# Attended values at another address, a regrouped last output, and earlier v sums in a windowed attention and feed-forward kernel

## The chip, the cores and the metric

One core of one Trainium2 chip. The time is the device time of one execution in microseconds (us); the profile is of one such execution, and its span runs from the first to the last instruction. Five engines work from queues of their own: PE (matrix products; its weight loads are listed apart as PEld), DVE, ACT, POOL, and SP, which here only issues DMA transfers.

## The reference

For each of 4 batches and 8 heads, 768 queries of 64 numbers attend to the keys nearer than 16 positions and, beside them, to 24 summaries of blocks of 32 positions (the maximum of the keys, the mean of the values). The result of all heads, 512 numbers per position, goes through a feed-forward layer:

```python
k_sum = k.reshape(B, H, nb, block, D).max(axis=3)
v_sum = v.reshape(B, H, nb, block, D).mean(axis=3)
...
a = a / (np.sum(a, axis=-1, keepdims=True) + 1e-09)
v_all = np.concatenate([v, v_sum], axis=2)
...
h = x @ w_in
r = np.maximum(h, 0.0)
g = s * (r * r) + b
return (g @ w_out).astype(np.float32)
```

`w_in` is 512 x 2048 and `w_out` 2048 x 512; the output has 3072 rows of 512.

## The kernel before, in words

**Chunks.** The 3072 rows are cut into 12 chunks of 256 rows (`T`), three to a batch. A chunk first needs its attention, which gives the attended values, transposed: four tiles of 128 x 256. They are split into an upper part `xh` in a format that the matrix unit takes in one pass, and a lower part `xl`, the rest. Each weight is split likewise into `wh` and `wl`.

**First products** (`hidden`, L460). For each of 16 steps `f` of the hidden layer, 12 products of 128 x 128 weights (stationary) with 128 x 256 attended values (moving): `wl` with `xh`, `wh` with `xl`, `wh` with `xh`, over four parts each. Two steps share a PSUM tile `ph`. The chain behind it (`activate`, `scaled`, `upper_rows`, `lower_rows`) makes `r` on ACT, scales it on POOL (L481), and splits it into `gh` and `gl` on DVE (L219, L492).

**Second products** (`project`, L504). For each step, two halves of rows (`t`, 128 rows each, PSUM tiles `po`), three products each: `gl` or `gh` stationary, 128 x 512 output weights moving. After step 15 `evict` copies each `po` to a tile `o` and sends it out (L514).

**The order of work** is a table `plan`: `then(step, order, ...)` appends a piece to a step of 1/16 chunk, and all engines get their instructions in that order. From chunk 2 on, first products are issued for four steps at once and second products for the four steps before, so PE alternates 48 first products and 24 second products. Each chunk boundary has a visit in which PE makes the values of the next chunk (`values`, L417) and the scores of the one after it (`scores`, L301).

**Sums of v** for the three later batches, made during the chunk before the batch's first: `load_v` brings v in six pieces (L165, SP), `v_sum` adds blocks on DVE (L172), `v_mean` scales on ACT (L178) into `vmean`, of which there is one buffer, and sends it by four small DMAs into `vsum` (L180, SP). `fill_v` on POOL (L263) copies `vsum` into the rows of `vw` that `values` reads. ACT runs its queue in order, and so does each of the others.

**Addresses.** Where tiles lie in a partition of SBUF, in bytes modulo 256, in the built programs of both kernels (the two buffers of a name separated by a comma):

| tile | role in products | before | with the change |
|---|---|---|---|
| xh and xl, each | moving in first products | 0, 0 | 192, 192 |
| wh, wl (rings) | stationary in first, moving in second products | 0 | 0 |
| gh and gl, each four | stationary in second products | 0 | 0 |
| r | between ACT, POOL, DVE | 0, 0 | 192, 224 |
| pr | between DVE and ACT | 192, 224 | 192, 64 |
| pT | moving in `values` | 192, 192 | 192, 192 |
| qk (four) | both sides of `scores` | 0, 160, 64, 224 | the same |

Of the kernel before, what the change touches and what calls it, by code (L numbers as in the profile page):

```python
# [11 lines left out]
F32 = mybir.dt.float32  # L12
# [7 lines left out]
P = 128  # L20
B, H, S, D = 4, 8, 768, 64
DM, DFF = 512, 2048
# [5 lines left out]
KR = WIN + NB  # L28
NSUB = 4
T = NSUB * SUB  # L30
NPAIR = H // 2
PER_B = S // T
NC = B * PER_B
NST = S // SUB
NKC = DM // P
NF = DFF // P
# [8 lines left out]
def windowed_attention_then_relu2_ffn(ctx, tc, qk, vwin, kt, vt, kq, vrow, wp, out):  # L45


    nc = tc.nc
# [4 lines left out]
    stage = ctx.enter_context(tc.tile_pool(name="stage", bufs=4))  # L53
    p2 = ctx.enter_context(tc.tile_pool(name="p2", bufs=2))
# [29 lines left out]
    def mask_of(st):  # L84
        return mask_first if st == 0 else mask_last if st == NST - 2 else mask_mid
# [3 lines left out]
    def at(step, order, fn, *args):  # L89
        plan[step].append((order, len(plan[step]), fn, args))  # L90
# [5 lines left out]
    for base, sign in ((0, 1), (BLOCK - 1, -1)):  # L96
        nc.gpsimd.affine_select(
            out=mean4[:, NB - 4 : NB], in_=mean4[:, NB - 4 : NB], compare_op=ALU.is_ge, fill=0.0,
            base=base, pattern=[[-sign * BLOCK, 4]], channel_multiplier=sign,
# [3 lines left out]
    w_raw, w_f, w_h, w_l, held = {}, {}, {}, {}, {}  # L103
# [113 lines left out]
    def copy(by_dve, out_, in_):  # L217
        if by_dve:
            nc.vector.tensor_copy(out_, in_)  # L219
        else:  # L220
            nc.scalar.copy(out_, in_)  # L221
# [7 lines left out]
    def place(c):  # L229
        return c // PER_B, c % PER_B  # L230
# [75 lines left out]
    def masked(c, p, j):  # L306
        _, ci = place(c)
        if j == 0 and c == 0:
            t = stage.tile([P, 4 * KR + 8], F32, name="pr0", tag="stage")
            pr_of[c, p] = t[:, : 4 * KR].rearrange("p (n k) -> p n k", k=KR)  # L310
            mn_of[c, p], sm_of[c, p] = t[:, 4 * KR : 4 * KR + 4], t[:, 4 * KR + 4 :]
        elif j == 0:
            if (c, p // 2) not in prs_of:
                prs_of[c, p // 2] = p2.tile([P, 8 * KR + 8], F32, name="pr", bufs=2)
                if turns_on_dve(c):
                    nc.gpsimd.memset(prs_of[c, p // 2][:, 8 * KR :], 0.0)
            t = prs_of[c, p // 2][:, 4 * KR * (p % 2) : 4 * KR * (p % 2 + 1)]
            pr_of[c, p] = t.rearrange("p (n k) -> p n k", k=KR)
            mn_of[c, p] = p2.tile([P, 4], F32, name="mn", bufs=4)
            sm_of[c, p] = p2.tile([P, 4], F32, name="sums", bufs=4)  # L320
        for e in range(2):
            n = 2 * e + j
            nc.vector.tensor_tensor_reduce(  # L323
                out=pr_of[c, p][:, n, :], in0=ps_of[c, p][e][:, j, :], in1=mask_of(NSUB * ci + 2 * j),
                scale=-1.0 / math.sqrt(D), scalar=3.0e38, op0=ALU.add, op1=ALU.min,
                accum_out=mn_of[c, p][:, n : n + 1],
            )
        if j == 1:
            ps_of.pop((c, p))
            qk_t.pop((c, p))  # L330
# [17 lines left out]
    prs_of, pTs_of = {}, {}  # L348

    def turns_on_dve(c):  # L350
        return c > 2
# [84 lines left out]
    ph_of, gg, po = {}, {}, {}  # L436
# [25 lines left out]
            )  # L462

    def activate(c, q, other=0):
        gg[c, q] = r = p2.tile([P, 2 * T], F32, name="r")
        ph = ph_of.pop((c, q))
        if other < 2:
            nc.scalar.activation(r, ph, AF.Relu)  # L468
        else:
            nc.vector.tensor_scalar(r, ph, 0.0, None, ALU.max)  # L470
        if other % 2:
            nc.vector.tensor_tensor(r, r, r, ALU.mult)
        else:
            nc.scalar.activation(r, r, AF.Square)  # L474
# [20 lines left out]
    def project(c, f):  # L495
        if f == 0:
            for t in range(T // P):
                pool, tag = ((ps_t, "pt"), (ps_v, "pav"))[t] if c == 1 else (ps_po, "po")
                po[c, t] = pool.tile([P, DM], F32, name="po", tag=tag)
        gh, gl = (g[:, (f % 2) * T : (f % 2 + 1) * T] for g in gg[c, f // 2])  # L500
        terms = [(gl, w_h[f]), (gh, w_l[f]), (gh, w_h[f])]
        for t in range(T // P):
            for n, (a, w) in enumerate(terms):
                nc.tensor.matmul(  # L504
                    po[c, t], a[:, t * P : (t + 1) * P], w[:, 512:],
                    start=(f == 0 and n == 0), stop=(f == NF - 1 and n == len(terms) - 1),
                )

    def evict(c, t, other=False):
        o = stage.tile([P, DM], F32, name="o", tag="stage")  # L510
        copy(other, o, po[c, t])
        bi, ci = place(c)
        r0 = bi * S + ci * T + t * P
        nc.sync.dma_start(out[r0 : r0 + P, :], o)  # L514


    LOAD, SPLIT, ATT, NEXT, TURN, WEIGHTS, HID, PE_ATT, CHAIN, VISIT, PROJ, EVICT = range(12)
# [29 lines left out]
    def of(fn, *more):  # L547
# [4 lines left out]
        "i": of(load_weights, "in"), "o": of(load_weights, "out"), "w": of(load_weights, "in", "out"),  # L552
        "u": load_unit, "x": load_values, "L": load_k,
        "W": keep_warm, "K": k_max, "k": fill_k, "Z": scores_of_maxima, "S": scores, "M": masked, "E": exps,
        "N": normalize, "T": transposes, "C": turned, "V": values, "U": values_of_means, "R": mean_of_rows,
        "F": mean_done, "t": fill_v, "X": attended, "y": attended_low, 
        "Ai": of(scale_weights, "in"), "Ao": of(scale_weights, "out"), "A": of(scale_weights, "both"),
        "Bi": of(convert_weights, "in"), "Bo": of(convert_weights, "out"), "D": of(convert_weights, "both"),
        "Y": hidden_part, "H": hidden, "J": activate, "G": scaled, "a": upper_rows, "b": lower_rows,
        "P": project, "O": evict, "h": upper_weights, "l": lower_weights,  # L560
    }
    ahead = set()
# [15 lines left out]
    def then(step, order, fn, *args):  # L578
        if (fn, args) not in ahead:
            at(step, order, fn, *args)  # L580

    for c in range(2, NC):
        bi, ci = place(c)
        for p in range(NPAIR):
            base, v_at = NF * (c - 1) - 1, (9, 10, 4, 5)[p]
            tr = 8 + 4 * (p // 2)
            lags = (1, 1, 1, 2, (12, 13, 11, 11)[p], tr, tr, 16, 17)
            m, e0, e1, n, fv, tr, tu, va, xa = (base + lag for lag in lags)
            if ci == 0:
                then(base - 12 + p, LOAD, load_k, bi, p)  # L590
                then(base - 7 + p, ATT, k_max, bi, p)
                if p < 2:
                    for third in range(3):
                        then(base + v_at - 5 + third, LOAD, load_v, bi, p, third)
                        then(base + v_at - 1 + third // 2, ATT, v_sum, bi, p, third)
                    then(base + v_at + 1, ATT, v_mean, bi, p)
            then(base - 6, LOAD, load_unit, c, p)
            then(base + v_at, LOAD, load_values, c, p)
            then(base - 2, ATT, fill_k, c, p)
            for j in range(2):  # L600
                then(base, VISIT, scores, c, p, j)
                then(m, NEXT if p < 2 else ATT, masked, c, p, j)
                then((e0, e1)[j], NEXT if p < 2 else ATT, exps, c, p, j)
            then(n, ATT, normalize, c, p)
            then(fv, ATT, fill_v, c, p)
            if turns_on_dve(c):
                for u in range(8):
                    a, k = divmod(u + 8 * (p % 2), 4)
                    then(base + TURN_AT[2 * p + u // 4], TURN, turned_blocks, c, p // 2, a, k)
            else:  # L610
                then(tr, PE_ATT, transposes, c, p)
                then(tu, CHAIN, turned, c, p)
            then(va, VISIT, values, c, p)
            if p % 2 == 0:
                then(xa, ATT, attended, c, p)
                then(xa, ATT, attended_low, c, p)
# [3 lines left out]
    for i in range(NF, NC * NF):  # L620
        c, f = divmod(i, NF)

        then(i - i % 4, HID, hidden, c, f)
        if f % 2:
            for stage_of in (activate, scaled, upper_rows, lower_rows):
                then(i, CHAIN, stage_of, c, f // 2)
        then((i + 4) | 3, PROJ, project, c, f)
        if f == NF - 1:
            for t in range(T // P):
                then((i + 4) | 3, EVICT, evict, c, t)  # L630
# [60 lines left out]
```

## Time and profile before

| what | us |
|---|---|
| median of 3 runs | 621.0 (620.56 to 621.52) |
| the profiled execution, its own time | 620.62 |
| its span | 618.9 |
| PE busy in the span | 608.4 |
| DVE busy | 418.7 |
| ACT busy | 276.6 |
| POOL busy | 138.0 |

PE is busy nearly throughout, so the places to look at are what one product costs and the few gaps. Busy times of matrix products overlap one another (the next starts while one still runs out), so the cost of a product is read from the distance of starts, or from a length of the chain divided by its count, not from its duration.

### The profile page before, as it was taken

The numbers are of one execution on the slowest core, as the hardware profiler recorded it, in microseconds if no ns is written. First come the engines' busy times: TensorE is split into PE (matmuls) and PEld (weight loads), VectorE is DVE, ScalarE is ACT, GpSimd is POOL, SyncE is SP. The second block draws the span as 40 slices with busy tenths as digits, with TensorE's granted clock in tenths as the row PEclk, the third lists the DMA queues.
The fourth block names the chain that finished last, engine by engine and source line by source line (L and its number), as shares of the span: only waits on it lengthen the run. The fifth ranks groups of instructions, "written<-read, shape, count | busy, mean of one in ns | idle before, by whom it ended". The sixth has DMA issues, their size and how long they took to land.

```text
span 618.9 us, 13522 instructions
## 1 busy us (share of the span) xinstructions
PE 608.4 (98%) x5240; PEld 551.3 (89%) x5240; DVE 418.7 (68%) x1126; ACT 276.6 (45%) x712; POOL 138.0 (22%) x275
## 2 busy tenths in 40 slices
PE   6999999999999999999999999999999999999997
PEld 5798999899889998998999899999998998999896
DVE  6999988689488278568758648947848827832211
ACT  5999997262352362263163154234235235223221
POOL 4420012211410411411131411321141051041110
PEclk9999999999999999999999999999999999999999
DMA  8998722026105017003503112500710500200000
GB/s 338 398 412 325 280 71 109 23 86 195 57 2 182 1 44 255 23 20 103 169 20 128 56 44 72 207 19 28 214 49 1 183 4 16 86 1 1 35 1 34
DMA packets 26993, 66.41 MB, mean 107 GB/s; under 512 B 3824, under 2 KB 3824, under 8 KB 26928
## 3 DMA queue, kind: packets, MB, share of 16 engines
q1 hardware_dynamic: 26928, 65.54, 29.9%
q8 instruction: 41, 0.67, 0.4%
q14 instruction: 24, 0.20, 0.1%
HBM read 59.09 MB, written 6.29 MB: 106 GB/s over the span
## 4 chain that ended last, share of the span: by engine, by line
PE 94%; ACT 3%; POOL 1%; DVE 1%; issue 1%; POOLq 0%; DVEq 0%; ACTq 0%
PE ph L460 44%; PE po L504 43%; PE pav L417 4%; PE ps L301 3%; ACT pr L336 2%; PE pt L379 0%; POOL vw L263 0%; PE ph L441 0%; DVE pr L346 0%; ACT pT L221 0%; ACT wraw L122 0%; ACT wraw L123 0%; POOL mask_first L73 0%; ACT vsum L221 0%; POOL mask_mid L73 0%
## 5 line engine op out<-in xcount | busy, mean ns | idle before, releaser
L481 POOL TENSOR_SCALAR r<-r,sb_col 128x512 f32<-128x512 f32 x85 | 68.9, 811 | 396.2 <-ACT r L474 281.2
L504 PE MATMUL po<-wh,gl 128*128 128x512 f32 x384 | 151.5, 395 | 0.0
L504 PE MATMUL po<-wl,gh 128*128 128x512 f32 x384 | 150.0, 391 | 0.0
L504 PE MATMUL po<-wh,gh 128*128 128x512 f32 x384 | 149.6, 389 | 0.0
L468 ACT ACTIVATE r<-ph 128x512 f32<-128x512 f32 x93 | 55.5, 597 | 209.9 <-PE ph L460 201.8
L219 DVE CAST gh<-r 128x512 fp32r<-128x512 f32 x88 | 38.3, 435 | 143.0 <-POOL r L481 140.3
L368 DVE STREAM_TRANSPOSE pT<-pr 32x256 f32<-32x256 f32 x288 | 125.5, 436 | 4.1
L460 PE MATMUL ph<-xl,wh 128*128 128x256 f32 x760 | 122.2, 283 | 0.0
L460 PE MATMUL ph<-xh,wh 128*128 128x256 f32 x760 | 122.1, 283 | 0.0
L460 PE MATMUL ph<-xh,wl 128*128 128x256 f32 x760 | 122.0, 283 | 0.0
L460 PEld LDWEIGHTS ph<-xh,wl 128*128 128x128 f32 x760 | 108.0, 191 | 4.3 <-issue 0.2
L460 PEld LDWEIGHTS ph<-xh,wh 128*128 128x128 f32 x760 | 104.9, 192 | 0.0
L460 PEld LDWEIGHTS ph<-xl,wh 128*128 128x128 f32 x760 | 104.8, 192 | 0.0
L504 PEld LDWEIGHTS po<-wh,gh 128*128 128x128 f32 x384 | 72.1, 188 | 15.5
L504 PEld LDWEIGHTS po<-wh,gl 128*128 128x128 f32 x384 | 72.3, 188 | 14.9 <-issue 1.0
L504 PEld LDWEIGHTS po<-wl,gh 128*128 128x128 f32 x384 | 72.3, 188 | 12.9
L336 ACT ACTIVATE pr<-pr,mn 128x120 f32<-128x120 f32 x176 | 67.0, 383 | 23.0 <-DVE mn L323 22.8
L492 DVE TENSOR_TENSOR gl<-r,gh 128x512 fp32r<-128x512 f32 x96 | 69.2, 721 | 4.1 <-ACT gh L221 1.3
L474 ACT ACTIVATE r<-r 128x512 f32<-128x512 f32 x92 | 58.1, 632 | 5.4 <-DVE r L470 2.5
L263 POOL COPY vw<-vsum 24x256 f32<-24x256 f32 x88 | 46.7, 565 | 37.1 <-DMA vsum<-vmean 16.4
L221 ACT COPY o<-po 128x512 f32<-128x512 f32 x23 | 13.5, 587 | 45.5 <-PE po L504 44.4
L346 DVE TENSOR_TENSOR pr<-pr,rs 128x480 f32<-128x480 f32 x48 | 32.1, 670 | 2.4 <-ACT pr L336 0.5
(88 smaller groups left out, 480.2 us busy)
## 6 DMA issues: line engine op xcount, KB each, us to landing
wraw<-in_wp_dram SPq DMA_DIRECT2D x32, 512.0 KB
qk<-in_qk_dram SPq DMA_DIRECT2D x44, 369.0 KB
vw<-in_vwin_dram SPq DMA_DIRECT2D x48, 256.0 KB
out_dram<-o SPq DMA_DIRECT2D x24, 256.0 KB
kraw<-in_kt_dram SPq DMA_DIRECT2D x12, 384.0 KB
vraw<-in_vt_dram SPq DMA_DIRECT2D x12, 252.0 KB
kq<-in_kq_dram SPq DMA_DIRECT2D x4, 512.0 KB
vraw<-in_vt_dram SPq DMA_DIRECT2D x6, 264.0 KB
```

Source lines behind the costliest of these rows:

```text
L219: nc.vector.tensor_copy(out_, in_)
L263: nc.gpsimd.tensor_copy(vw_t[c, p][WIN:KR, e], vsum[bi][WIN : WIN + NB, 2 * p + e, :].unsqueeze(1).to_broadcast([NB, NSUB, D]),)
L336: nc.scalar.activation(pr, pr, AF.Exp, bias=mn_of[c, p][:, n : n + 1], scale=-1.0, accum_out=sm_of[c, p][:, n : n + 1])
L346: nc.vector.tensor_tensor(pr, pr, rs.unsqueeze(2).to_broadcast([P, 4, KR]), ALU.mult)
L368: nc.vector.transpose(to[BLOCK * k : BLOCK * (k + 1), :, rows], src)
L417: nc.tensor.matmul(oi, vw[:KR, e, i, :], pi[:KR], start=True, stop=True)
L460: nc.tensor.matmul(ph, w[:, kc * P : (kc + 1) * P], x[:, kc], start=(n == 0), stop=(n == len(terms) - 1))
L468: nc.scalar.activation(r, ph, AF.Relu)
L474: nc.scalar.activation(r, r, AF.Square)
L481: (nc.vector if other else nc.gpsimd).tensor_scalar(g, g, s_col, b_col, ALU.mult, ALU.add)
L492: nc.vector.tensor_tensor(gl, g, gh.bitcast(F32), ALU.subtract)
L504: nc.tensor.matmul(po[c, t], a[:, t * P : (t + 1) * P], w[:, 512:], start=(f == 0 and n == 0), stop=(f == NF - 1 and n == len(terms) - 1),)
```

## The change

Three edits. (1) The tile `pr` is 24 numbers longer and the tile `r` 8; nothing reads or writes the added columns. By the order in which the pool places its tiles, `xh` and `xl` thereby start at 192 instead of 0 modulo 256, and `gh`, `gl` and what follows stay where they were modulo 256. (2) For the last chunk's steps 12 to 15 the second products are issued by row half: all 12 of the first half, then all 12 of the second; each output half-tile is copied in two halves of 256 columns, the first by ACT and the second by DVE, with a DMA for each (`project_last`). (3) `v_sum` and `v_mean` stand one step sooner in the table; the loads stand where they were.

```diff
@@ masked
-                prs_of[c, p // 2] = p2.tile([P, 8 * KR + 8], F32, name="pr", bufs=2)
+                prs_of[c, p // 2] = p2.tile([P, 8 * KR + 32], F32, name="pr", bufs=2)
                 if turns_on_dve(c):
-                    nc.gpsimd.memset(prs_of[c, p // 2][:, 8 * KR :], 0.0)
+                    nc.gpsimd.memset(prs_of[c, p // 2][:, 8 * KR : 8 * KR + 8], 0.0)
@@ activate
-        gg[c, q] = r = p2.tile([P, 2 * T], F32, name="r")
+        gg[c, q] = r = p2.tile([P, 2 * T + 8], F32, name="r")[:, : 2 * T]
@@ new
+    def project_last():
+        for t in range(T // P):
+            for f in range(NF - 4, NF):
+                gh, gl = (g[:, (f % 2) * T + t * P : (f % 2) * T + (t + 1) * P] for g in gg[NC - 1, f // 2])
+                for n, (a, w) in enumerate(((gl, w_h[f]), (gh, w_l[f]), (gh, w_h[f]))):
+                    nc.tensor.matmul(
+                        po[NC - 1, t], a, w[:, 512:], start=False, stop=(f == NF - 1 and n == 2),
+                    )
+            o = stage.tile([P, DM], F32, name="o", tag="stage")
+            r0 = (NC - 1) * T + t * P
+            for n in range(2):
+                cols = slice(n * DM // 2, (n + 1) * DM // 2)
+                copy(n, o[:, cols], po[NC - 1, t][:, cols])
+                nc.sync.dma_start(out[r0 : r0 + P, cols], o[:, cols])
@@ the table
-                        then(base + v_at - 1 + third // 2, ATT, v_sum, bi, p, third)
-                    then(base + v_at + 1, ATT, v_mean, bi, p)
+                        then(base + v_at - 2 + third // 2, ATT, v_sum, bi, p, third)
+                    then(base + v_at, ATT, v_mean, bi, p)
@@ the table, second products
+        if i >= NC * NF - 4:
+            if f == NF - 1:
+                then((i + 4) | 3, PROJ, project_last)
+            continue
         then((i + 4) | 3, PROJ, project, c, f)
```

On DVE, in the chunk before each of the three batches (vhalf: sums of v; pT: turned probabilities; gh, gl: the split rows of the chain), a row before:

```order
L368 STREAM_TRANSPOSE pT<-pr 32x8x32 x4
L172 TENSOR_REDUCE vhalf<-vraw 96x22
L172 TENSOR_REDUCE vhalf<-vraw 96x21
L368 STREAM_TRANSPOSE pT<-pr 32x8x32 x4
L219 CAST gh<-r 128x512
L492 TENSOR_TENSOR gl<-r,gh 128x512
L172 TENSOR_REDUCE vhalf<-vraw 96x21
L172 TENSOR_REDUCE vhalf<-vraw 96x22
L172 TENSOR_REDUCE vhalf<-vraw 96x21
L368 STREAM_TRANSPOSE pT<-pr 32x8x32 x4
L172 TENSOR_REDUCE vhalf<-vraw 96x21
```

and now:

```order
L172 TENSOR_REDUCE vhalf<-vraw 96x22
L172 TENSOR_REDUCE vhalf<-vraw 96x21
L368 STREAM_TRANSPOSE pT<-pr 32x8x32 x4
L172 TENSOR_REDUCE vhalf<-vraw 96x21
L172 TENSOR_REDUCE vhalf<-vraw 96x22
L172 TENSOR_REDUCE vhalf<-vraw 96x21
L368 STREAM_TRANSPOSE pT<-pr 32x8x32 x4
L219 CAST gh<-r 128x512
L492 TENSOR_TENSOR gl<-r,gh 128x512
L172 TENSOR_REDUCE vhalf<-vraw 96x21
```

Two sums pass one group of transposes, three pass another and one split, and the last sum passes a group; that split stands three sums later.

On SP, the DMA queue, at the same place (vw: windows of v; qk: queries and keys of the next chunk):

```order
 L252 DMA vw<-in_vwin_dram 128x512
-L252 DMA vw<-in_vwin_dram 128x512 x2
+L252 DMA vw<-in_vwin_dram 128x512
+L180 DMA vsum<-vmean 24x64 x4
+L252 DMA vw<-in_vwin_dram 128x512
 L245 DMA qk<-in_qk_dram 128x738 x4
-L180 DMA vsum<-vmean 24x64 x8
+L180 DMA vsum<-vmean 24x64 x4
```

The first four small DMAs now stand ahead of one load of `vw` and the four loads of `qk`; the other four stay behind them. On ACT the two `vmean` instructions, which had one pair of `activate` between them, now stand directly one behind the other, ahead of that pair.

On PE, the last 24 second products of the program (po_7148 is the first half of rows, po_7149 the second), the end of the list before:

```order
L504 MATMUL po_7148<-wh_1513,gl_7328 128x512
L504 MATMUL po_7148<-wl_1552,gh_7326 128x512
L504 MATMUL po_7148<-wh_1513,gh_7326 128x512
L504 MATMUL po_7149<-wh_1513,gl_7328 128x512
L504 MATMUL po_7149<-wl_1552,gh_7326 128x512
L504 MATMUL po_7149<-wh_1513,gh_7326 128x512
```

and now:

```order
L514 MATMUL po_7149<-wh_1513,gl_7328 128x512
L514 MATMUL po_7149<-wl_1581,gh_7326 128x512
L514 MATMUL po_7149<-wh_1513,gh_7326 128x512
L514 MATMUL po_7149<-wh_1513,gl_7328 128x512
L514 MATMUL po_7149<-wl_1552,gh_7326 128x512
L514 MATMUL po_7149<-wh_1513,gh_7326 128x512
```

The first half's last product stood three ahead of the end, and stands twelve ahead of it now.

## The prediction, made before the changed kernel was run

> **What bounds the kernel now.** I read the page first, then the chain that ended last, then the starts of single products in narrow stretches of the timeline, and the waits around the chunk boundaries last.
>
> ```profile
> span 618.9 us, 13522 instructions
> ...
> PE 608.4 (98%) x5240; PEld 551.3 (89%) x5240; DVE 418.7 (68%) x1126; ACT 276.6 (45%) x712; POOL 138.0 (22%) x275
> ...
> PE 94%; ACT 3%; POOL 1%; DVE 1%; issue 1%; POOLq 0%; DVEq 0%; ACTq 0%
> ```
>
> PE carries 94% of the chain, so a change counts by what it does to the rate of products, or to the few places where PE stands. From chunk 2 on the chain repeats pieces of this kind (start, length, engine and line, count):
>
> ```profile
> 301.57 5.47 PE po L504 x24
> 307.04 5.75 PE ph L460 x48
> 312.79 2.02 PE pav L417 x64
> 314.80 1.80 PE ps L301 x64
> ```
>
> A second product (512 moving columns) costs 5.47 us / 24 = 227.9 ns, a first product (256 columns) 5.75 us / 48 = 119.8 ns. The 256 columns of difference cost 108.1 ns, so 119.8 - 108.1 = 11.7 ns of each product do not go with its columns. Whatever the address of the moving operand can give in first products is in these 11.7 ns. Is it a fixed price, or does it move? These are the weight loads beside the products, and the starts of the first few products of a group:
>
> ```profile
> L460 PEld LDWEIGHTS ph<-xh,wl 128*128 128x128 f32 x760 | 108.0, 191 | 4.3 <-issue 0.2
> L460 PEld LDWEIGHTS ph<-xh,wh 128*128 128x128 f32 x760 | 104.9, 192 | 0.0
> ...
> L504 PEld LDWEIGHTS po<-wh,gh 128*128 128x128 f32 x384 | 72.1, 188 | 15.5
> ```
>
> ```profile
> 576.06 0.28 PE L460 MATMUL ph<-xh,wl 128*128 128x256 f32 x1
> ...
> 576.17 0.40 PE L460 MATMUL ph<-xh,wl 128*128 128x256 f32 x2
> ...
> 604.25 0.40 PE L504 MATMUL po<-wh,gl 128*128 128x512 f32 x1
> 604.49 0.40 PE L504 MATMUL po<-wl,gh 128*128 128x512 f32 x1
> 604.72 0.39 PE L504 MATMUL po<-wh,gh 128*128 128x512 f32 x1
> ...
> 606.09 0.39 PE L504 MATMUL po<-wh,gh 128*128 128x512 f32 x1
> 606.32 0.39 PE L504 MATMUL po<-wh,gl 128*128 128x512 f32 x1
> ```
>
> It moves. The same 128x128 load takes 188 ns beside a second product and 191 to 192 beside a first one. The first product of a group is followed after 0.11 us, the rest at 0.12; and second products, 0.23 apart when settled, start 0.24 apart where the group begins. All these operands lie at 0 modulo 256. So the distance depends on how two streams that PE reads at once, the moving operand and the next weights, stand to each other in time. A shift of one stream's address is a shift of that kind.
>
> **Edit 1, the address, by parts.** It adds no instruction and moves none. It touches all 2280 first products at L460 (three rows of 760) and 24 at L441: 2304. *Bounds:* below, the whole unexplained 11.7 ns goes, 2304 x 11.7 = 27 us gained; above, first products settle as badly against their best as second products do at a group's start, 0.24 against 0.23, so +10 ns and 23 us lost. *Value:* the nearest row is the weight load, which is made in both groups and is 188 without and 191.5 with the conflict (mean of the L460 rows). I take it that the new phase ends that part and no more: 3.5 ns x 2304 = 8.1 us gained. Against a dependence on addresses as such speaks this piece, in which transposes follow one another at 110 ns though their stationary operand `pr` starts at four different places modulo 256:
>
> ```profile
> 94.10 0.44 PE pt L379 x4
> ```
>
> But these stream 128 columns, half of what a first product streams beside a load of the same kind, so the two streams may simply not meet.
>
> The Trainium skill, TensorE: Matmul & The Clock Gate, section "Step-by-step: what each phase is for", says that the array reads moving operand and weights through two independent SBUF ports, so that the next load takes nothing from the running product; by it edit 1 is worth 0. The rows of 188 and 192 ns for one and the same load do not agree with it.
>
> `r` and one buffer of `pr` move to other addresses too. `pr` lies at 192 and 224 today, and its readers show one duration for both (minimum, median, maximum):
>
> ```profile
> L368 DVE STREAM_TRANSPOSE pT<-pr x288: 425/436/442, 134.8 to 543.3; 32x256 f32<-32x256 f32 x144
> ...
> L346 DVE TENSOR_TENSOR pr<-pr,rs x48: 657/659/823, 9.7 to 521.8; 128x480 f32<-128x480 f32 x48
> ```
>
> So 0 for these. Were DVE's 0.43 us splits a tenth slower, the 2 to 7 us in which DVE waits before them would hide it.
>
> **Edit 3, v sums.** At the one boundary where PE stands today, before chunk 3:
>
> ```profile
> 151.84 9.85 SPq L180 DMA_DIRECT2D vsum<-vmean  x8
> ...
> 154.92 0.85 DVE L172 TENSOR_REDUCE vhalf<-vraw 96x21 f32<-96x672 f32 x1
> ...
> 157.71 0.26 ACT L178 ACTIVATE vmean<-vhalf 96x64 f32<-96x64 f32 x1 [4.75 <-DMA vsum<-vmean]
> ...
> 161.91 1.43 POOL L263 COPY vw<-vsum 24x256 f32<-24x256 f32 x4 [8.02 <-DMA vsum<-vmean]
> ```
>
> ```profile
> 159.06 2.89 PE ph L460 x24
> ...
> 164.97 1.47 POOL vw L263 x2
> ...
> 166.49 1.61 PE pav L417 x46
> 168.10 1.80 PE ps L301 x64
> 169.90 1.12 PE po L504 x4
> ```
>
> From the start of the group of first products to the first second product it is 169.90 - 159.06 = 10.84 us here, and 5.75 + 2.02 + 1.80 = 9.57 in the undisturbed boundary above: PE loses 1.27 us to POOL's copies, which began at 161.91 because the second `vmean` had waited 4.75 us for the landing of the first. With the change the first four small DMAs stand ahead of the `qk` loads. On DVE the last sum ends about 1.8 us sooner (one group of four transposes, 1.78, now behind it), near 154.0; the first `vmean` goes at about 148.9 and has landed by then, so the second goes near 154.2 instead of 157.7. Its DMAs, today 161.91 - 157.97 = 3.9 us to landing, may queue behind `qk` loads that SP now issues 1.5 us later (SP holds them until the first `vmean`); I expect POOL to start near 159, its last two copies to end near 163.5, and PE to need them near 165. **1.2 us gained**; 0 if the `qk` loads delay the second half by all that was won, 1.27 at most. What is late next: the pair of `activate` that stood between the two `vmean`, at 151.72 to about 154.2, and one split on DVE, three sums of 0.85 later:
>
> ```profile
> 149.61 0.43 DVE L219 CAST gh<-r 128x512 fp32r<-128x512 f32 x1
> 150.07 0.69 DVE L492 TENSOR_TENSOR gl<-r,gh 128x512 fp32r<-128x512 f32 x1
> ```
>
> It would end near 153.2. The group of second products that reads it starts at 153.59, and reads this pair in its second half, 2.7 us later; about 3 us of cover. Without it, the price would be what exceeds those 3 us, at three boundaries. At the other two PE did not stand, and gains nothing there.
>
> **Edit 2, the end.** The same 24 products, in another order; the split of their last pair must be ready six products into the group instead of twelve, 1.4 us sooner; it is some 3 us early.
>
> ```profile
> 614.68 1.27 ACT L221 COPY o<-po 128x512 f32<-128x512 f32 x2 [8.63 <-PE po L504]
> ...
> 615.29 1.01 SPq L514 DMA_DIRECT2D out_dram<-o  x2
> ...
> L221 ACT CAST xh<-pav 128x256 fp32r<-128x256 f32 x5 | 1.8, 369 | 0.8 <-PE pav L417 0.8
> ...
> L219 DVE CAST xh<-pav 128x256 fp32r<-128x256 f32 x3 | 1.3, 418 | 0.0
> ...
> 617.00:617.40 0.40, 0.00 (x0) 0.00 (x0) 0.00 (x0) 0.00 (x0) 0.00 (x0) 1.00 1.05 410
> 617.40:617.80 0.40, 0.00 (x0) 0.00 (x0) 0.00 (x0) 0.00 (x0) 0.00 (x0) 1.00 0.21 72
> ```
>
> The last copy ends at 614.68 + 1.27 = 615.95. Two halves side by side, from about 615.36, take 0.37 and 0.42 by the rows of like copies out of PSUM, so they end at 615.78. SP must issue two DMAs, one behind the other, about 0.34 each, so the last issue comes at 616.1, not sooner than today's, which ends at 616.30. But it carries 128 KB behind another 128 KB, where today two of 256 KB queue at 410 GB/s until about 617.6; the last bytes should go out about 0.3 us sooner. **0.3 us gained**; bounds: 0.6 gained (all 256 KB of the first half gone), 0.2 lost (two issues more expensive than the bytes).
>
> **Sum.** 8.1 + 1.2 + 0.3 = 9.6 us: the span falls from 618.9 to 609.3. The execution's own time was 620.62, 0.4 below the median of the runs; from the median it is 621.0 - 9.6 = **611.4 us**.
>
> **Rivals.**
>
> *Nothing from the address.* The extra 11.7 ns is a price of changing weights, and goes on as it is. For it: settled groups keep one distance over hundreds of products, and the transposes do not mind their addresses. Against it: 188 against 192 ns, and 0.11 against 0.12. Time: 621.0 - 1.5 = 619.5.
>
> *More from the address.* Each first product then settles at the distance of its group's first, 0.11 instead of 0.12; I reckon 7 ns: 2304 x 7 = 16.1 us, with the other edits 603.4. Against it: the weights of 128 columns must still come in, 110 ns in the transposes.
>
> *A worse phase, slower.* The streams meet more often than today, as second products do at a group's start. At +4 ns per first product it costs 9.2 us, and 621.0 - 1.5 + 9.2 = 628.7. It decides from 1.5 us / 2304 = 0.65 ns per product on. For it: the settled distance of second products is the smallest of theirs, so today's phase may be the good one there. Against it: in first products the settled distance is the larger one.
>
> *The boundary again.* With shorter groups of first products, PE reaches its boundaries sooner, and the copies on POOL could bind at chunks 6 and 9 too. Per chunk only 8.1 / 12 = 0.7 us are won, against over 2 us by which edit 3 brings POOL forward, so this takes away at most tenths; it is in the range.
>
> **How the numbers follow.** Forecast 0.45, nothing 0.28, more 0.10, slower 0.17. Within 0.2% means within 1.24 us, about what a measurement of this kernel can tell. The 1.5 us of the second case are just over that, so I put 0.6 of it to faster: 0.45 + 0.10 + 0.17 = 0.72; same 0.11; slower 0.17. The forecast's own range is 605 to 617; for 8 in 10 it must hold "more" and "nothing" and the smaller losses: 602 to 623.
>
> **What would show it.** Right: groups of 48 first products in the chain at about 5.58 us instead of 5.75, with weight loads of 188 ns there; 5.47 for second products as before; the piece before chunk 3 near 9.5 us, with no POOL in it; the last copy about 0.17 sooner and less than 2.95 us from it to the span's end. Wrong: 5.75 (address without effect) or more (worse phase); new waits of PE for `gl` or `vw` at chunks 3, 6 or 9; a last DMA that starts later than today's by more than its smaller size saves.

## The result and the profile after

The changed kernel takes 613.6 us (median) against 620.8 of the kernel before, measured beside it: a ratio of 0.988, 95% interval 0.986 to 0.990, 7.2 us less. It is faster, by three quarters of the 9.6 us that were forecast. A fourth execution took 849.7 us at a granted clock of 0.658, where the other three had 0.999 to 1.0, and does not enter the ratio. The profiled execution has 613.58 us and a span of 611.9, 7.0 below the span before.

From the page of the changed kernel, the same lines as before:

```profile
span 611.9 us, 13540 instructions
...
PE 602.6 (98%) x5240; PEld 546.4 (89%) x5240; DVE 418.3 (68%) x1128; ACT 275.5 (45%) x712; POOL 137.1 (22%) x275
```

PE is still busy for 98% of a shorter span: the products themselves became cheaper. The chain that ended last (start, length, engine and line, count), at the first whole group behind the startup, at the boundary before chunk 3 and at the end:

```profile
124.70 5.46 PE ph L460 x48
...
146.71 5.65 PE ph L460 x48
152.36 5.44 PE po L504 x24
157.80 5.65 PE ph L460 x48
163.45 2.02 PE pav L417 x64
165.47 1.80 PE ps L301 x64
...
597.38 5.44 PE po L504 x24
602.82 5.45 PE po L514 x24
```

48 first products take 5.65 us instead of 5.75, so 117.7 ns each instead of 119.8, but for one group, the one at 124.70, which takes 5.46; 24 second products that follow first ones take 5.44 instead of 5.47. From the start of the first products to the end of the scores there are 9.47 us here, with no POOL in the chain, where 10.84 stood before; 1.27 of the difference is the stand of PE and 0.10 the shorter group.

The whole difference, by places that both chains have (the kernel before first): up to the first values after the preparation of the weights 117.04 and 116.33, 0.7 us less; from there to the first second product after the boundary before chunk 3, 52.86 and 50.94, 1.9 less, of which 1.27 are the stand; from there to the last but one group of second products, 434.52 and 430.11, 4.4 less; from there to the end 14.48 and 14.52, nothing. That makes 7.0. The 0.7 us of the startup can't be put down to an edit: in two executions of one kernel (the weights at 64, below) the first values began at 116.04 and at 117.45.

The weight loads (groups by line and shape; the number before the last bar is the mean in ns):

```profile
L460 PEld LDWEIGHTS ph<-xh,wl 128*128 128x128 f32 x760 | 106.3, 189 | 4.6 <-issue 0.3
L460 PEld LDWEIGHTS ph<-xh,wh 128*128 128x128 f32 x760 | 103.4, 190 | 0.0
L460 PEld LDWEIGHTS ph<-xl,wh 128*128 128x128 f32 x760 | 102.6, 189 | 0.0
```

They are 2 ns shorter than before, but not at the 188 ns that they need beside a second product. Whether that is what the products gained is tested below. And the end (timeline; the brackets give idle time before an instruction and what ended it):

```profile
607.87 0.39 PE L514 MATMUL po<-wh,gh 128*128 128x512 f32 x1
608.29 0.37 ACT L221 COPY o<-po 128x256 f32<-128x256 f32 x1 [2.35 <-PE po L514]
608.69 0.81 SPq L522 DMA_DIRECT2D out_dram<-o  x2
608.70 0.42 DVE L219 COPY o<-po 128x256 f32<-128x256 f32 x1 [2.29 <-ACT o L221]
```

```profile
609.50:609.90 0.40, 0.00 (x0) 0.00 (x0) 0.00 (x0) 0.00 (x0) 0.00 (x0) 1.00 0.87 310
```

The two half copies do not run side by side: DVE waits for ACT, and ends 0.83 us after ACT began, where one whole copy took 0.59. The last two columns are the busy share of the DMA engines and GB/s. The last two transfers of 128 KB are issued one behind the other, the second only after DVE's copy, and the engines are busy for 0.87 of this stretch at 310 GB/s, where the two transfers of 256 KB before had kept them at 1.05 and 410. From the end of the last copy to the end of the span it is 2.78 us here and 2.95 before.

### The profile page after: what moved, and what is told of

It is laid out like the page before. It is cut to its first block, busy times and chain, and to the rows that moved or that the text cites. A ratio compares the mean times of both kernels' runs of the same rounds, so it can differ in the third digit from the quotient of the medians.

```text
span 611.9 us, 13540 instructions
## 1 busy us (share of the span) xinstructions
PE 602.6 (98%) x5240; PEld 546.4 (89%) x5240; DVE 418.3 (68%) x1128; ACT 275.5 (45%) x712; POOL 137.1 (22%) x275
## 4 chain that ended last, share of the span: by engine, by line
PE 84%; ACT 8%; DMA 3%; DVE 3%; issue 1%; SPq 0%; ACTq 0%; DVEq 0%
PE ph L460 38%; PE po L504 38%; PE pav L417 4%; PE ps L301 3%; DMA wraw<-in_wp_dram 3%; ACT wraw L122 2%; ACT wraw L123 2%; ACT pr L336 1%; DVE wf L132 1%; PE po L514 1%; ACT r L474 1%; PE pt L379 1%; ACT r L479 1%; ACT r L468 0%; ACT wh L221 0%
## 5 line engine op out<-in xcount | busy, mean ns | idle before, releaser
L504 PE MATMUL po<-wh,gl 128*128 128x512 f32 x376 | 147.9, 393 | 0.2 <-DVE gl L492 0.2
L504 PE MATMUL po<-wl,gh 128*128 128x512 f32 x376 | 146.5, 390 | 0.0
L504 PE MATMUL po<-wh,gh 128*128 128x512 f32 x376 | 146.4, 389 | 0.0
L460 PE MATMUL ph<-xl,wh 128*128 128x256 f32 x760 | 120.3, 281 | 0.0
L460 PE MATMUL ph<-xh,wh 128*128 128x256 f32 x760 | 120.3, 281 | 0.0
L460 PEld LDWEIGHTS ph<-xh,wl 128*128 128x128 f32 x760 | 106.3, 189 | 4.6 <-issue 0.3
L460 PEld LDWEIGHTS ph<-xl,wh 128*128 128x128 f32 x760 | 102.6, 189 | 0.0
L504 PEld LDWEIGHTS po<-wh,gl 128*128 128x128 f32 x376 | 70.6, 188 | 14.6 <-issue 1.4
L504 PEld LDWEIGHTS po<-wl,gh 128*128 128x128 f32 x376 | 70.6, 188 | 12.4
L221 ACT COPY o<-po 128x512 f32<-128x512 f32 (+1 forms) x23 | 13.1, 568 | 45.7 <-PE po L504 35.6
```

Source lines behind the costliest of these rows:

```text
L460: nc.tensor.matmul(ph, w[:, kc * P : (kc + 1) * P], x[:, kc], start=(n == 0), stop=(n == len(terms) - 1))
L504: nc.tensor.matmul(po[c, t], a[:, t * P : (t + 1) * P], w[:, 512:], start=(f == 0 and n == 0), stop=(f == NF - 1 and n == len(terms) - 1),)
```

## The experiments

**The three edits apart.** First the address alone, on the kernel before:

```diff
-                prs_of[c, p // 2] = p2.tile([P, 8 * KR + 8], F32, name="pr", bufs=2)
+                prs_of[c, p // 2] = p2.tile([P, 8 * KR + 32], F32, name="pr", bufs=2)
...
-        gg[c, q] = r = p2.tile([P, 2 * T], F32, name="r")
+        gg[c, q] = r = p2.tile([P, 2 * T + 8], F32, name="r")[:, : 2 * T]
```

> Edit 1 alone on the kernel before. My theory (what the address gives is spent on the products themselves): groups of 48 first products at 5.65 us instead of 5.75 in the chain, groups of 24 second products behind them at 5.44 instead of 5.47, the piece before chunk 3 still with its stand of 1.3 us; about 5.8 us less than before, 615 us. Rival (the gain needs edit 3, since POOL's copies take the place of what PE wins): 5.65 too, but new stands of PE at chunks 3, 6 and 9, and under 4.5 us less.

Measured: 616.3 us beside 621.0, ratio 0.9923 (0.9908 to 0.9938), 4.8 us less (3.9 to 5.7). The chain has the lengths of the changed kernel, and the stand before chunk 3 is still there:

```profile
305.52 5.65 PE ph L460 x48
...
314.99 5.66 PE po L504 x24
```

```profile
PE pav L417 <- POOL vw L263: 0.7, 2, 0.5
```

No new stand at the later boundaries: the rival, in which POOL's copies take what PE wins, falls; the row above is the wait before chunk 3 alone. The 5.8 expected lies just outside the interval. It includes the 0.7 us of the startup, which this run does not show: its first values begin at 117.31, against 116.33 with the whole change and 117.04 before.

Then the v sums alone:

```diff
-                        then(base + v_at - 1 + third // 2, ATT, v_sum, bi, p, third)
-                    then(base + v_at + 1, ATT, v_mean, bi, p)
+                        then(base + v_at - 2 + third // 2, ATT, v_sum, bi, p, third)
+                    then(base + v_at, ATT, v_mean, bi, p)
```

> Edit 3 alone. My theory: the stand before chunk 3 goes (from 10.84 to 9.57 us between the start of the first products and the first second product), nothing else changes: 1.2 to 1.3 us less, 619.6 us. Rival (it is worth something only with shorter products): 0.

Measured: 619.5 us, ratio 0.9977 (0.9967 to 0.9986), by which it is 1.4 us less. The chain before chunk 3:

```profile
159.11 5.75 PE ph L460 x48
164.86 2.02 PE pav L417 x64
166.88 1.80 PE ps L301 x64
168.68 3.42 PE po L504 x14
```

168.68 - 159.11 = 9.57 us, what an undisturbed boundary takes. As expected.

And the end alone, `project_last` and its place in the table on the kernel before:

```diff
+        if i >= NC * NF - 4:
+            if f == NF - 1:
+                then((i + 4) | 3, PROJ, project_last)
+            continue
```

> Edit 2 alone. What I believe after the first comparison: the copy of the second half of columns on DVE starts only when ACT's has ended, so the last copy ends later by about 0.2 us, and the smaller last transfer gives about as much back: within 0.1 us of before. Rival (as forecast): 0.3 us less.

Measured: 620.6 us, ratio 0.9996 (0.9986 to 1.0006). The end shows the same two copies in a row (the profiled execution took 622.8 us; its first values began 2.0 us later than before):

```profile
617.53 0.37 ACT L221 COPY o<-po 128x256 f32<-128x256 f32 x1 [2.35 <-PE po L514]
617.93 0.42 DVE L219 COPY o<-po 128x256 f32<-128x256 f32 x1 [2.29 <-ACT o L221]
```

This edit is worth nothing that can be measured. Why DVE waits stands in the built program's list, with waits shown, and could have been read there before the prediction:

```
L219 COPY o_7383<-po_7149 128x256 [waits DMAHW1_49,Activation_49]
```

The second of the two waits is for ACT's copy of the first half. It stands there too when each half is given a tile `o` of its own (built, not run), so it is the common PSUM tile for which the program puts the two readers in a row.

**What about the address?** The theory so far: two streams that PE reads at once, the moving operand and the next weights, hinder each other, and what counts is how they stand to each other. So the same difference made from the other side should do the same: weights 64 further, attended values back at 0.

```diff
-    mean4 = const.tile([P, 2 * NB - 4], F32, name="mean4")
+    mean4 = const.tile([P, 2 * NB - 4 + 16], F32, name="mean4")[:, : 2 * NB - 4]
...
-        gg[c, q] = r = p2.tile([P, 2 * T + 8], F32, name="r")[:, : 2 * T]
+        gg[c, q] = r = p2.tile([P, 2 * T], F32, name="r")[:, : 2 * T]
```

(`mean4` lies ahead of all weights, so 64 more bytes there move everything behind it.)

> Weights (and all that lies between) moved by 64 bytes, attended values back at 0 modulo 256, so that the moving operand stands to the weights as 0 to 64, which is the same difference as 192 to 0; edits 2 and 3 are in. Theory of the difference (two streams that PE reads at once meet): first products in groups of 5.65 us, as with the change. Rival (the moving operand's own address modulo 256 decides): 5.75 us, as before.

Measured: 609.4 us in one execution, and a chain that neither expected:

```profile
302.19 5.47 PE ph L460 x48
...
317.17 5.47 PE ph L460 x48
322.64 5.49 PE po L504 x24
```

```profile
L460 PEld LDWEIGHTS ph<-xl,wh 128*128 128x128 f32 x760 | 101.0, 188 | 0.0
```

First products at 5.47 us / 48 = 114.0 ns, their weight loads at 188 ns, the value that they have beside second products. Second products, whose moving operand is now at 64 and whose stationary one is at 0, are a little dearer: 5.49. Either the weights' own address counts, or the same difference has more than one outcome.

Two more places for the attended values, by the lengths of `pr` and `r` (8 and 16 more numbers in `pr` instead of 24, the rest in `r`):

```diff
-                prs_of[c, p // 2] = p2.tile([P, 8 * KR + 32], F32, name="pr", bufs=2)
+                prs_of[c, p // 2] = p2.tile([P, 8 * KR + 16], F32, name="pr", bufs=2)
```

> The changed kernel with the attended values at 64 instead of 192 modulo 256, weights at 0. Theory 'one good place': the distance of settled first products depends on where the stream starts, and 64 is no better than 0: groups of first products at 5.75 us or above. Rival 'any start off a multiple of 256': 5.65 us, as at 192.

> The same at 128. Theory 'one good place': neither 5.75 nor 5.65 is fixed, something between or above. Rival 'any start off a multiple of 256': 5.65 us.

Measured: at 64 groups of 5.66 us, 615.3 us in all; at 128 groups of 5.76, 620.2, the time of the kernel before beside it, though edits 2 and 3 are in. So 64 is nearly as good as 192, 128 no better than 0; neither theory of these two runs holds for both. A group and a row of the weight loads, first at 64, then at 128:

```profile
303.95 5.66 PE ph L460 x48
L460 PEld LDWEIGHTS ph<-xh,wh 128*128 128x128 f32 x760 | 102.8, 188 | 0.0
```

```profile
294.91 5.76 PE ph L460 x48
L460 PEld LDWEIGHTS ph<-xh,wh 128*128 128x128 f32 x760 | 104.2, 189 | 0.0
```

The loads are as short as with the weights at 64, 188 ns, and yet a product takes 117.9 ns and not 114.0; at 128 they take 189 and a product 120.0. So what a load lasts is not what a product pays.

Then the stationary operand of second products, `gh` and `gl` at 64 (`r` 16 numbers longer than in the kernel before; and the scratch for DMA descriptors 1024 bytes shorter, which makes room and moves all tiles by a multiple of 256):

> The changed kernel (values at 192, weights at 0) with gh and gl, the stationary operand of second products, at 64 instead of 0. Theory 'the place of the stationary operand counts by itself' (after the weights at 64 brought first products to 113.5 ns, below the 117.7 of the same difference): groups of second products clearly under 5.44 us, at 5.2 to 5.35. Rival (second products are bound by their 512 moving columns, which hide the load): 5.44 us.

Measured: 617.3 us. Second products become dearer, 5.59 or 5.60. More telling is what happened to the first products, whose operands lie as in the changed kernel, values at 192 and weights at 0, throughout this run:

```profile
126.01 5.66 PE ph L460 x48
...
137.27 5.46 PE ph L460 x48
...
320.51 5.46 PE ph L460 x48
325.97 5.59 PE po L504 x24
331.56 5.66 PE ph L460 x48
```

Groups of 5.46 and of 5.65 us alternate within a chunk; of the 40 whole groups in the chain, 20 are of the one and 20 of the other length (5.65 and 5.66 together). The same addresses have two settled states. The place in the chunk does not choose between them: chunk 2 begins with 5.66 (at 126.01), the later ones with 5.46. That the group before chooses, by how it leaves the two streams, fits this alternation, but is not shown.

Then the weights at 128:

> Weights at 128, attended values, gh and gl at 0. Theory 'the place of the weights counts by itself': first products at about 5.47 us as with the weights at 64, second products (now with their moving operand at 128) near 5.49. Rival 'the difference counts': the same value as the attended values at 128 with weights at 0 gives, whatever that is.

Measured: 622.7 us; second products 5.57 to 5.60, and first ones in two lengths, which change from chunk to chunk:

```profile
306.88 5.69 PE ph L460 x48
...
322.17 5.76 PE ph L460 x48
```

Of 42 whole groups 16 take 5.76, as with the values at 128, and 25 take 5.69 or 5.70. None takes 5.47, so not every place of the weights off a multiple of 256 helps. Two runs to decide between differences and absolute addresses: all operands of first and second products 64 further (with the shorter scratch again), so with the differences of the changed kernel, and the weights at 192, which gives first products the difference 64 of the run with the values at 64.

> Weights at 64, gh and gl at 64, attended values at 0: every difference between two streams as in the changed kernel, every address 64 further. Theory 'differences, and two settled states': since nothing differs but the absolute address, groups of first products at 5.65 and of second at 5.44 us, as with the change; about 613 us. Rival 'the absolute address of the weights': first products at 5.47 us as with the weights at 64 alone, 609 us or less.

> Weights at 192, attended values, gh and gl at 0: moving minus stationary is 64 in first products, as with the attended values at 64. Theory of differences: first products at 5.66 us or in a second, shorter state under 5.5; rival (absolute): something else, 5.75 or above.

The first, with these operands 64 further, took 614.1 us, and its chain is that of the changed kernel:

```profile
303.58 5.65 PE ph L460 x48
...
313.05 5.66 PE po L504 x24
318.72 5.65 PE ph L460 x48
```

The second took 620.7 us, with first products at 5.65 (5.66 with the values at 64), and second products, at a difference of 192, at 5.60, what `gh` at 64 had given, which is the same difference:

```profile
294.93 5.65 PE ph L460 x48
300.58 5.60 PE po L504 x24
```

No run needs absolute addresses. Equal differences give equal lengths of first products, or one of two: 5.46 or 5.65 us at 192, 5.69 or 5.76 at 128. Second products agree to 0.04 us (at a difference of 0 from 5.44 to 5.48, behind different first ones). The kernel with the weights at 64 was then run once more with a time:

> The kernel with the weights at 64 once more, timed, because its one execution was shorter than both kernels: 609.4 us, a ratio of 0.981 to the kernel before, with first products in groups of 5.47 us again. If the shorter state is reached by chance, some executions would show 5.65 us and 613.

Measured: 609.7 us (608.9 to 610.9), ratio to the kernel before 0.981 (0.979 to 0.983). It beats both kernels, the changed one by about 4 us, though not measured beside it. In the chain of the profiled execution (610.9 us) 32 of the 36 whole groups of first products take 5.47 us, and the other four, all of chunk 3, take 5.65 or 5.66:

```profile
174.29 5.66 PE ph L460 x48
179.94 5.51 PE po L504 x24
...
222.96 5.47 PE ph L460 x48
228.43 5.49 PE po L504 x24
```

In the first execution of the same kernel chunk 3 took 5.46 and 5.47. So the shorter state is not sure: one program falls into either, for a chunk at a time, at the same addresses and in the same order. The rival of the boundary shows here in small: with shorter groups PE stands for `vw` again before chunk 3 (0.8 us in the first execution), but not before chunks 6 and 9.

```profile
PE pav L417 <- POOL vw L263: 0.3, 1, 0.3
```

Last, a step finer than 64, the weights at 32 (a tile of 56 numbers ahead of the others in the same pool, and the shorter scratch, bring the values back to 0):

> Weights at 32, attended values, gh and gl at 0: a difference of 224 in first products and of 32 in second ones, between the places tried so far (steps of 64). Theory 'the streams meet by pieces of 64 bytes': 32 does as 0 or as 64 does, first products in groups of 5.75, 5.65 or 5.47 us, second ones of 5.47 to 5.49. Rival 'finer pieces': values that none of the runs had, second products below 5.44 among them.

Measured: 621.7 us, first products 5.68 and second 5.60 (the line numbers of this kernel are one higher).

```profile
306.56 5.68 PE ph L461 x48
...
327.53 5.60 PE po L505 x24
```

Second products at 32 pay 5.60, at 0 and at 64 no more than 5.51: the place counts in finer pieces than 64 bytes. Neither length is far from those of other runs (5.69 at 128, 5.60 at 192), and no group of second products came below 5.44, as the rival had thought possible. All runs together, by the difference of addresses, moving minus stationary, modulo 256, and the length of a group in us (second products where they follow first ones). That lengths repeat every 256 bytes is taken for granted there; no run was made to test it.

| run | first products: difference | 48 take | second products: difference | 24 take |
|---|---|---|---|---|
| before | 0 | 5.75 | 0 | 5.47 |
| change, and all 64 further | 192 | 5.65, and 5.46 once in the change | 0 | 5.44 |
| values at 64 | 64 | 5.66 | 0 | 5.48 |
| values at 128 | 128 | 5.76, and 5.69 or 5.70 once each | 0 | 5.48 |
| gh and gl at 64 | 192 | 5.46 or 5.65 | 192 | 5.59 or 5.60 |
| weights at 64 | 192 | 5.47, in one chunk 5.65 | 64 | 5.49, in that chunk 5.51 |
| weights at 128 | 128 | 5.69 to 5.76 | 128 | 5.57 to 5.60 |
| weights at 192 | 64 | 5.65 | 192 | 5.60 |
| weights at 32 | 224 | 5.68 | 32 | 5.60 |

## Why the prediction was right, and where its sizes were off

The forecast, faster by way of the products, came out; of the 9.6 us, 7.2 were measured. Term by term:

**The address**: 8.1 us forecast; 5.1 measured by the chain from the first values on (1.9 and 4.4, less the 1.27 of the stand), 4.8 with its interval of 3.9 to 5.7 in the run with this edit alone. Right was that the distance of products moves with how the starts of the two streams stand to each other: neither side's own address counts. The group that was forecast at 5.58 us took 5.65. The mis-sized step was "the new phase ends that part and no more: 3.5 ns". A product went from 119.8 to 117.7 ns, 2.1 of the 3.5; 40 groups of 48 behind the startup make 4.0 us of that, and the one group of 5.46 another 0.2. The rest came from a place that I had costed at nothing: second products that follow first ones no longer start 0.24 us apart before they settle, and 30 such groups at 0.03 us give 0.9.

The yardstick of that step does not hold either. I took the 3.5 ns from the weight loads, which went from 191 or 192 to 189 or 190 ns; that products gained about as much is luck, as far as the runs show. Loads of 188 ns stand beside first products of 114.0 ns with the weights at 64, of 117.9 with the values at 64 and of 118.3 with the weights at 32. Luck is also the place: nothing in the prediction speaks for 192 rather than 128, and at 128 this edit gains nothing.

**No effect of the address**, the rival by the Trainium skill (TensorE: Matmul & The Clock Gate, "Step-by-step: what each phase is for"), fell. By the rule that the load takes nothing from the running product, the three edits would have given 619.5; and moving only `gh` and `gl`, which PE only ever loads, changed 24 second products from 5.44 to 5.59 or 5.60 us.

**More from the address** had named 0.11 us, the distance of a group's first products, as a state in which a whole group could settle, and had spoken against it. The changed kernel reaches it in one of its 40 groups behind the startup, and the weights at 64 in most, at 114 ns. **A worse phase** exists for second products: at a difference of 32 or 192 they take 5.60 us, 0.13 more than in the kernel before. For first products, of which the prediction spoke, no run showed one: 5.76 us at most against 5.75.

**v sums**: 1.2 forecast, 1.27 by the chain, 1.4 (0.9 to 2.0) in the run alone. POOL's first copy began at 159.11, forecast "near 159", and its last two at 162.17 ended at 163.63, forecast "near 163.5":

```profile
159.11 2.13 POOL L263 COPY vw<-vsum 24x256 f32<-24x256 f32 x6 [3.66 <-DMA vsum<-vmean]
161.34 0.77 POOL L481 TENSOR_SCALAR r<-r,sb_col 128x512 f32<-128x512 f32 x1
162.17 1.46 POOL L263 COPY vw<-vsum 24x256 f32<-24x256 f32 x2
```

The delayed split on DVE stayed covered: no wait of PE for `gl` appears at the boundaries.

**The end**: 0.3 forecast, nothing measured. The step that failed is "two halves side by side". They run one behind the other, because the program makes DVE wait for ACT at the PSUM tile that both read; the last copy ends 0.24 us later than one whole copy would, and with the smaller last transfer the span ends 0.17 us sooner after it. The wait was written in the program's list beforehand.

Two things stay open: why the difference of the starts counts at all, and what chooses between the two states at 192 and at 128. That the two streams hinder each other where PE reads them is the reading which the prediction began with, and no run contradicts it; but no run shows the place where they would meet. The runs show the lengths and what they cost.

## What to carry to other kernels

Where a product's distance exceeds what its columns explain, compare the first few of a group with the settled ones: if they differ at the same addresses, try other differences between the starts of the moving operand and of the next weights, modulo 256. Judge such a trial by the length of whole groups in the chain, which one execution gives to 0.01 us, and not by the time alone nor by the duration of the weight loads; and go through all groups of more than one execution, since the same addresses can settle in two ways. Before counting on two engines to empty one tile side by side, read the waits in the program's list.

## What the runs showed of the hardware that was not expected

Operands that are only shifted by 32 to 192 bytes change settled first products between 113.8 and 120.0 ns (5.46 and 5.76 us for 48) and second ones between 226.7 and 233.3 (5.44 and 5.60 for 24), as means of whole groups, with no instruction changed and a granted clock of 0.999 to 1.0 in each of these runs. One and the same pair of addresses gave 5.46 and 5.65 us in turn in a single execution. The duration of a weight load does not tell which: 188 ns beside first products of 114.0, 117.9 and 118.3 ns.
